# Issuing the attention scores of a head pair as one run of sixteen matmuls instead of two runs of eight

## The chip, the cores and the metric

The kernel runs on one core of a Trainium2 chip. The metric is the time of one execution on the device, in microseconds (us); the median of several executions is quoted, with the lowest and the highest.

## The reference

Two layers in a row. The first is block attention: per head, a sorting matrix `P` (8x8, made by five Sinkhorn steps) mixes the eight blocks of keys and values, then each block attends to itself. The second is a residual MLP whose tokens are mixed too.

```python
# attention: B=4, H=8, S=768, D=64; eight blocks of 96 tokens
k_sorted = np.einsum('bhij,bhjcd->bhicd', P, k_b)
v_sorted = np.einsum('bhij,bhjcd->bhicd', P, v_b)
scores = scale * np.matmul(q_b, k_sb.transpose(0, 1, 2, 4, 3))     # 96x96 per block
attn = softmax(scores); x = np.matmul(attn, v_sb)
# MLP: x is (4, 768, 512)
a1 = alpha1 * x + beta1
tok = np.einsum('ts,bsd->btd', w_tok, a1)                          # token mixing
u = x + lam * tok
ch = np.maximum((alpha2 * u + beta2) @ w_ch1, 0.0) @ w_ch2         # 512 -> 2048 -> 512
out = u + lam * ch
```

## The kernel before

Attention of batch b and the MLP of batch b-1 are emitted one after the other, and a scheduler at build time interleaves them on each engine. TensorE's trace shows the order that was built (batch 1 of before: score runs of 1, 15 and six of 8 in both). The names to know: `sc_ps` are scores, `et` their exps (ScalarE), `x_ps` the value products, `h_ps` the first MLP layer, `ch_ps` its second, `tok_ps` the token mixing. PSUM is split into a pool of two large tiles (`psA`: scores, value products, key and value mixing) and one of four small ones (`psB`: the MLP).

```python
psA = ctx.enter_context(tc.tile_pool(name="psA", bufs=2, space=bass.MemoryType.PSUM))
psB = ctx.enter_context(tc.tile_pool(name="psB", bufs=4, space=bass.MemoryType.PSUM))
# ... cut ...
def emit_scores(b, h4, g, spins=0):                # h4: head pair, g: half of the blocks
    sps = psa([128, 2, 4, 128], FT, "sc_ps")
    # ... cut ...
    for ii, i in enumerate(blocks):                # four blocks
        for h2 in range(2):                        # two heads: rows 0 to 63 and 64 to 127
            rows = slice(h2 * 64, (h2 + 1) * 64)
            pe.matmul(sps[0:BLK, h2, ii, 0:BLK], kT[rows, h4 * NB + i, :],
                      qT[rows, h4, :, i * 16:(i + 1) * 16], start=True, stop=True)
    et = att.tile([BLK, 2, 4, BLK], F16, name="et", tag="et", bufs=4)
    act.activation(et..., sps..., AF.Exp, scale=scale)      # arguments cut
    return et

def emit_attention(b):
    # ... cut ...
    def gather(lo, hi):                            # 96-row blocks into the 128-row layout
        for a in range(3):
            dve.tensor_copy(x128[96:128, a:a + 4:3, lo:hi], xs[32 * a:32 * a + 32, :, lo:hi])

    prev = [emit_scores(b, 0, g) for g in range(2)]
    for h4 in range(1, H4):
        cur = [emit_scores(b, h4, g) for g in range(2)]
        emit_pv(b, h4 - 1, prev, x128, xs)         # value products, then normalised by VectorE
        prev = cur
        if h4 == H4 - 1:
            gather(0, 384)
    emit_pv(b, H4 - 1, prev, x128, xs)
    gather(384, C)

def moe_start(b):                                  # cut to its end
    for kt in range(NT):
        pool.tensor_scalar(u32[kt][:], b1lB[:], rs[:, kt:kt + 1], None, op0=ALU.mult)
        moe_add(b, kt)                             # GpSimd: u = x128 + u

for b in range(1, B):                              # cut to what matters
    emit_attention(b)
    if b == 1:
        moe_ch(0, 0, (2,))
    else:
        moe_h(b - 1, 0)
        moe_ch(b - 1, 0)
    moe_h(b - 1, 1)                                # 64 matmuls
    moe_a(b)                                       # moe_start, token mixing (36 matmuls), transposes
    moe_ch(b - 1, 1)
```

The softmax here doesn't subtract the row's maximum and nothing guards it: scores larger than these inputs give would overflow.

Of the kernel before, what the change touches and what calls it, by code (L numbers as in the profile page):

```python
# [7 lines left out]
FT = mybir.dt.float32  # L8
# [8 lines left out]
def kernel(  # L17
# [23 lines left out]
    NB = sort_net.shape[-1]  # L41
    BLK = S // NB
# [30 lines left out]
    pe = Engine(nc.tensor)  # L73
    dve = Engine(nc.vector)
    act = Engine(nc.scalar)
# [9 lines left out]
    def psa(shape, dtype, name):  # L85
        return psA.tile(shape, dtype, name=name, tag="psA")
# [42 lines left out]
    qT_of = {}  # L129
# [84 lines left out]
    def spin(ps, n):  # L214
        src = ident16[:].unsqueeze(1).to_broadcast([128, 4, 128])
        for _ in range(n):
            pe.matmul(ps, ident16[:], src, start=True, stop=True)
# [104 lines left out]
    kT_of = {}  # L322
# [30 lines left out]
    def mix_k(b, share=(4, 0, 4), gs=range(3)):  # L353
        raw = raw_of[(b, 0)]
        rhs = bigP[b][:].rearrange("p g i -> p (g i)")
        if b not in kT_of:
            kT_of[b] = att.tile([128, H4 * NB, BLK], F16, name="kT", tag="kT", bufs=2)
        kv_ = kT_of[b][:].rearrange("p c (par th tp) -> p th c par tp", th=2, par=2)
        for g in gs:
            kps = psa([128, 8, 128], FT, "k_ps")  # L360
            for tp in range(8):
                t0 = (8 * g + tp) * 128
                pe.matmul(kps[:, tp, :], raw[:, t0:t0 + 128], rhs, start=True, stop=True)
            for par in range(2):
                for h2 in range(2):
                    src = kps[par * 64:(par + 1) * 64, :, h2 * 64:(h2 + 1) * 64].rearrange(
                        "p n (th c) -> p th c n", th=2
                    )
                    dst = kv_[h2 * 64:(h2 + 1) * 64, :, :, par, 8 * g:8 * g + 8]
                    if 2 * par + h2 < share[g]:  # L370
                        dve.tensor_copy(dst, src)
                    else:
                        act.copy(dst, src)

    def mix_heads(kv, h4, out, copies):

# [32 lines left out]

    x_of = {}  # L410

    def emit_scores(b, h4, g, spins=0):
        kT = kT_of[b]
        qT = qT_of[b]
        blocks = ((0, 1, 2, 6), (3, 4, 5, 7))[g] if b == 0 else range(4 * g, 4 * g + 4)
        sps = psa([128, 2, 4, 128], FT, "sc_ps")
        spin(sps[:, 0, :, :].rearrange("p i x -> p (i x)"), spins)
        for ii, i in enumerate(blocks):
            for h2 in range(2):
                rows = slice(h2 * 64, (h2 + 1) * 64)  # L420
                pe.matmul(
                    sps[0:BLK, h2, ii, 0:BLK], kT[rows, h4 * NB + i, :], qT[rows, h4, :, i * 16:(i + 1) * 16],
                    start=True, stop=True,
                )
        et = att.tile([BLK, 2, 4, BLK], F16, name="et", tag="et", bufs=4)
        act.activation(
            et[:].rearrange("p a i (r kt) -> p (a i) r kt", kt=NT),
            sps[0:BLK].rearrange("p a i x -> p (a i) x")[:, :, 0:BLK].rearrange("p n (kt r) -> p n r kt", kt=NT),
            AF.Exp, scale=scale,
        )  # L430
        return et

    def emit_pv(b, h4, ets, x128, xs):
        for g in range(2):
            xall = psa([128, 4, 256], FT, "x_ps")
            xps = xall[0:BLK]
            flat = ets[g][:].rearrange("p a i x -> p (a i x)")
            for ii in range(4):
                i = 4 * g + ii
                for h2 in range(2):  # L440
                    at = (h2 * 4 + ii) * BLK
                    rows = min(128, 8 * BLK - at)
                    pe.matmul(
                        xall[0:rows, ii, h2 * GRP:h2 * GRP + D + 1], flat[:, at:at + rows],
                        Vs[b % NV][:, (2 * h4 + h2) * NB + i, 0:D + 1],
                        start=True, stop=True,
                    )
            recip = att.tile([BLK, 4, 2], FT, name="recip", tag="recip", bufs=3)
            sums = xps[:, :, D:D + GRP + 1:GRP]
            vals = xps[:, :, 0:2 * GRP].rearrange("p i (a g) -> p i a g", a=2)[:, :, :, 0:D]  # L450
            dve.reciprocal(recip[:], sums)
            for lo, hi in ((0, 4),) if g == 0 else ((0, 2), (2, 4)):
                i = 4 * g + lo
                cols = slice(h4 * 128, (h4 + 1) * 128)
                dst = x128[0:BLK, i:i + hi - lo, cols] if i < 6 else xs[:, :, cols]
                dve.tensor_tensor(
                    dst.rearrange("p i (a d) -> p i a d", d=D), vals[:, lo:hi],
                    recip[:, lo:hi].unsqueeze(3).to_broadcast([BLK, hi - lo, 2, D]), ALU.mult,
                )

    def pv_tiles(h4, g, et, spins=0):

# [21 lines left out]
    def emit_attention(b):  # L484
        x128 = moep.tile([128, NT, C], F16, name="x128", tag="x128", bufs=2)
        xs = moep.tile([BLK, 2, C], F16, name="xs", tag="xs", bufs=1)
        x_of[b] = x128

        def gather(lo, hi):
            for a in range(3):  # L490
                dve.tensor_copy(x128[96:128, a:a + 4:3, lo:hi], xs[32 * a:32 * a + 32, :, lo:hi])

        prev = [emit_scores(b, 0, g) for g in range(2)]
        for h4 in range(1, H4):
            cur = [emit_scores(b, h4, g) for g in range(2)]
            emit_pv(b, h4 - 1, prev, x128, xs)
            prev = cur
            if h4 == H4 - 1:
# [3 lines that stand above are left out]
# [171 lines left out]
    def sc0(h4, g, spins=0):  # L673
        ets[(h4, g)] = emit_scores(0, h4, g, spins)
# [83 lines left out]
    for kk in range(2):  # L758
        moe_ch(0, 0, (kk,))
        mix_k(1, gs=((0, 1), (2,))[kk])  # L760
        for h4 in range(2 * kk, 2 * kk + 2):
            turn_q(1, h4, dve.tensor_copy)
    pe.fixed = False
    for b in range(1, B):
        if b > 1:
            if b > 2:
                cross_q(b)
            mixing_matrices(b)
            mix_v(b)
            if b == 2:  # L770
                opened = pool.tensor_copy(gate[:], Vs[0][0:1, 0, 0:2])
                with tc.issue_after(opened.ins):
                    load_q(3)
                    load_raw(3, 1)
                    load_raw(3, 0)
            mix_k(b)
# [6 lines that stand above are left out]
        moe_h(b - 1, 1)  # L783
        moe_a(b)
        moe_ch(b - 1, 1)
        if b == 1:
            load_q(2)
            cross_q(2)
# [33 lines left out]
```

## Time and profile before

| | before |
|---|---|
| time, 3 runs | 269.02 us (268.73 to 269.4) |
| profiled execution | 268.56 us, granted clock 1.00 |
| span in the trace | 266.8 us |
| TensorE busy | 257.3 us (96%) |
| stretch from the first MLP matmul | 219.80 us |

The page of the profile of before, cut to four lines: the span, the busy times (PE is TensorE, PEld its weight loads, DVE VectorE, ACT ScalarE, POOL GpSimd), the chain that ended last by engine, and one group of instructions (count, busy us and mean ns, then idle time before them).

```profile
span 266.8 us, 5147 instructions
...
PE 257.3 (96%) x2049; PEld 141.6 (53%) x2059; DVE 154.8 (58%) x333; ACT 125.8 (47%) x232; POOL 92.6 (35%) x100
...
PE 89%; ACT 4%; DVE 4%; issue 1%; DMA 1%; DVEq 0%; ACTq 0%
...
L65 PE MATMUL h_ps<-a2T,W1p 128*128 128x384 bf16 x512 | 93.4, 326 | 0.2
```

TensorE is the limit nearly everywhere (96% busy, 89% of the chain). The mean of 326 ns is the length of one matmul's record. What a matmul costs the stream is the distance to the next start, 162 ns for an h matmul, so everything below is read start to start.

The timeline of TensorE before, in the middle of batch 3's attention (start, length, engine, operation, output and inputs, count):

```profile
188.76 1.47 PE L65 MATMUL h_ps<-a2T,W1p 128*128 128x384 bf16 x8
190.16 0.38 PE L65 MATMUL sc_ps<-qT,kT 64*96 64x96 f16 x8
190.47 0.50 PE L65 MATMUL h_ps<-a2T,W1p 128*128 128x384 bf16 x2
190.90 0.38 PE L65 MATMUL sc_ps<-qT,kT 64*96 64x96 f16 x8
191.21 0.34 PE L65 MATMUL h_ps<-a2T,W1p 128*128 128x384 bf16 x1
191.50 0.41 PE L65 MATMUL x_ps<-Vs,et 96*128 96x65 f16 x8
```

Scores come in runs of eight and use 64 rows of the array (`64*96`); all their neighbours use 96 or 128. From an h matmul to the first score takes 256 ns instead of 162. From the last score to the next h matmul takes 138.

### The profile page before, as it was taken

What the parts mean: (1) busy time and instruction counts of PE and PEld (TensorE: products, weight loads), DVE (VectorE), ACT (ScalarE), POOL (GpSimd) and SP (SyncE); (2) the same over time, 40 slices, a digit from 0 to 9 for tenths busy, and PEclk for the clock granted to TensorE, in tenths of its full rate; (3) what the DMA queues carried; (4) which work ended last, traced back from release to release, by engine and by line L of the source; (5) the groups of instructions that cost most, each with busy time, mean ns of one, the idle gap of its engine ahead of it and who ended that gap; (6) DMA issues with size and microseconds to landing.
All of it is one profiled execution on the core that took longest, in us unless ns stands there. A gap on an engine that the chain in (4) does not pass through costs nothing.

```text
span 266.8 us, 5147 instructions
## 1 busy us (share of the span) xinstructions
PE 257.3 (96%) x2049; PEld 141.6 (53%) x2059; DVE 154.8 (58%) x333; ACT 125.8 (47%) x232; POOL 92.6 (35%) x100
## 2 busy tenths in 40 slices
PE   7799999999999999999999999999999999999993
PEld 3467745565565444554565444554565445545542
DVE  6878687639567966722585867704675962042033
ACT  3376767642585312980375404970474305505600
POOL 8524789103585615008918125002409000000000
PEclk9999999999999999999999999999999999999999
DMA  6999999989999544499996342492200422012012
GB/s 80 183 208 252 206 211 207 209 209 118 206 165 146 115 83 120 115 83 95 207 196 135 61 100 80 118 109 51 81 1 2 86 71 79 2 39 79 2 39 79
DMA packets 62423, 30.88 MB, mean 116 GB/s; under 512 B 48888, under 2 KB 58112, under 8 KB 62400
## 3 DMA queue, kind: packets, MB, share of 16 engines
q0 software_dynamic: 23024, 15.60, 39.1%
q1 hardware_dynamic: 39376, 14.96, 32.7%
q8 instruction: 16, 0.26, 0.4%
q14 instruction: 7, 0.06, 0.1%
HBM read 32.78 MB, written 8.65 MB: 155 GB/s over the span
## 4 chain that ended last, share of the span: by engine, by line
PE 89%; ACT 4%; DVE 4%; issue 1%; DMA 1%; DVEq 0%; ACTq 0%
PE ch_ps L65 31%; PE h_ps L65 30%; PE tok_ps L65 12%; PE x_ps L65 5%; PE sc_ps L65 4%; ACT kT L65 2%; PE v_ps L65 2%; PE k_ps L65 1%; PE q_ps L65 1%; ACT et L65 1%; DVE csum L65 1%; DVE P L65 1%; PE m_ps L65 1%; DVE rsum L65 1%; PE wtok_ps L65 1%
## 5 line engine op out<-in xcount | busy, mean ns | idle before, releaser
L65 PE MATMUL h_ps<-a2T,W1p 128*128 128x384 bf16 x512 | 93.4, 326 | 0.2
L65 ACT ACTIVATE hTa<-h_ps 128x384 bf16<-128x384 f32 x96 | 45.9, 492 | 67.7 <-PE h_ps L65 66.6
L65 PE MATMUL ch_ps<-W2p,hTa 128*128 128x512 bf16 (+2 forms) x290 | 65.9, 370 | 0.5
L65 PEld LDWEIGHTS <-W1p 128*128 128x128 bf16 x512 | 47.5, 98 | 30.3 <-issue 0.9
L65 DVE TENSOR_TENSOR ch_ps<-ch_ps,lamB 128x512 f32<-128x512 f32 (+2 forms) x25 | 16.9, 676 | 62.8 <-PE ch_ps L65 60.1
L65 POOL TENSOR_SCALAR u<-b1lB,rs 128x512 f32<-128x512 f32 x18 | 28.9, 1612 | 64.7 <-DVE ost L65 60.1
L65 PEld LDWEIGHTS <-hTa 128*128 128x128 bf16 x300 | 28.7, 98 | 32.4
L65 PE MATMUL tok_ps<-x,w_tokT 128*128 128x512 f16 x144 | 32.1, 379 | 0.0
L65 POOL TENSOR_TENSOR u<-x,u 128x512 f32<-128x512 f16 x22 | 25.4, 1190 | 18.2 <-DVE x L65 17.3
L65 ACT ACTIVATE et<-sc_ps 96x768 f16<-96x768 f32 x32 | 24.9, 807 | 11.7 <-PE sc_ps L65 11.7
L65 ACT CAST u<-u 128x512 f16<-128x512 f32 x24 | 14.8, 618 | 25.7 <-DVE u L65 25.7
L65 PE MATMUL ch_ps<-W2p,hTb 128*128 128x512 bf16 (+2 forms) x100 | 25.0, 371 | 0.0
L65 PEld LDWEIGHTS <-w_tokT 128*128 128x128 f16 x180 | 14.8, 97 | 16.1
L65 DVE TENSOR_TENSOR tok_ps<-tok_ps,a1lB 128x512 f32<-128x512 f32 x24 | 16.6, 693 | 7.7 <-PE tok_ps L65 7.6
L65 DVE CAST kT<-k_ps 64x512 f16<-64x512 f32 x24 | 16.5, 688 | 3.4 <-PE k_ps L65 3.0
L65 DVE TENSOR_TENSOR x<-x_ps,recip 96x512 f16<-96x512 f32 (+2 forms) x32 | 17.6, 554 | 0.9
L65 DVE TENSOR_TENSOR u<-tok_ps,u 128x512 f32<-128x512 f32 x24 | 16.4, 689 | 1.7
L65 ACT ACTIVATE hTb<-h_ps 128x384 bf16<-128x384 f32 x32 | 15.3, 497 | 3.8 <-PE h_ps L65 3.4
L65 DVE TENSOR_TENSOR ost<-ch_ps,u 128x512 f32<-128x512 f32 (+2 forms) x25 | 16.6, 665 | 0.6
L65 POOL DMA_DIRECT2D qn<-in_q_dram x18 | 15.4, 872 | 4.2 <-PE q_ps L65 3.4
L65 PEld LDWEIGHTS <-hTb 128*128 128x128 bf16 x100 | 9.6, 98 | 10.9
L65 PEld LDWEIGHTS <-et 96*128 96x128 f16 (+2 forms) x288 | 12.4, 99 | 4.6 <-issue 1.2
(95 smaller groups left out, 214.0 us busy)
## 6 DMA issues: line engine op xcount, KB each, us to landing
out_dram<-ost SPq DMA_DIRECT2D x23, 192.0 KB, 2.2
raw<-in_v_dram POOLq DMA_DIRECT2D x8, 384.0 KB, 8.2
raw<-in_k_dram POOLq DMA_DIRECT2D x8, 384.0 KB, 10.7
vscr<-vA SPq DMA_DIRECT2D x6, 384.0 KB, 4.4
Vs<-vscr SPq DMA_DIRECT2D x6, 384.0 KB, 7.5
W1p<-in_moe_w_ch_dram POOLq DMA_DIRECT2D x4, 512.0 KB, 10.5
W2p<-in_moe_w_ch_dram POOLq DMA_DIRECT2D x4, 512.0 KB, 18.6
qn<-in_q_dram POOLq DMA_DIRECT2D x12, 128.0 KB, 5.8
```

The costliest lines, as they stand in the source:

```text
L65: ins = getattr(self.eng, name)(*args, **kwargs)
```

## The change

The intent is to enter and leave runs of 64-row matmuls half as often. Both PSUM tiles of a head pair are taken first, sixteen score matmuls are issued over them, and then the two exps. The first score waits until both tiles are free (`freed`), and the others are chained to it. Batch 0 keeps its order.

```diff
+    def emit_pair(b, h4):
+
+        pair = [psa([128, 2, 4, 128], FT, "sc_ps") for _ in range(2)]
+        last = None
+        for g in range(2):
+            for ins in score(b, h4, range(4 * g, 4 * g + 4), pair[g]):
+                if last is None:
+                    behind(ins, freed[b], mybir.DependencyClass.Sync)
+                else:
+                    behind(ins, (last,), mybir.DependencyClass.NoSync)
+                last = ins
+        return [emit_exp(ps, b) for ps in pair]
 ... cut: freed[b] is set by the key copies, by each exp and by each normalisation;
 ... cut: emit_scores becomes score (the matmuls) and emit_exp (the exp) ...
-        prev = [emit_scores(b, 0, g) for g in range(2)]
+        prev = emit_pair(b, 0)
         for h4 in range(1, H4):
-            cur = [emit_scores(b, h4, g) for g in range(2)]
+            cur = emit_pair(b, h4)
```

More of the change, by code (lines that the diff above doesn't have):

```diff
@@ L360, in mix_k @@
             kps = psa([128, 8, 128], FT, "k_ps")
+            copies = []
             for tp in range(8):
@@ L370, in mix_k @@
                     if 2 * par + h2 < share[g]:
-                        dve.tensor_copy(dst, src)
+                        ins = dve.tensor_copy(dst, src)
                     else:
-                        act.copy(dst, src)
+                        ins = act.copy(dst, src)
+                    copies.append(ins)
+            freed[b] = copies
     def mix_heads(kv, h4, out, copies):
@@ L410, with score @@
     x_of = {}
-    def emit_scores(b, h4, g, spins=0):
-        kT = kT_of[b]
-        qT = qT_of[b]
-        blocks = ((0, 1, 2, 6), (3, 4, 5, 7))[g] if b == 0 else range(4 * g, 4 * g + 4)
-        sps = psa([128, 2, 4, 128], FT, "sc_ps")
-        spin(sps[:, 0, :, :].rearrange("p i x -> p (i x)"), spins)
+    def score(b, h4, blocks, sps):
         for ii, i in enumerate(blocks):
@@ L420, in emit_scores, with behind, emit_exp @@
                 rows = slice(h2 * 64, (h2 + 1) * 64)
-                pe.matmul(
-                    sps[0:BLK, h2, ii, 0:BLK], kT[rows, h4 * NB + i, :], qT[rows, h4, :, i * 16:(i + 1) * 16],
-                    start=True, stop=True,
-                )
+                yield pe.matmul(
+                    sps[0:BLK, h2, ii, 0:BLK], kT_of[b][rows, h4 * NB + i, :],
+                    qT_of[b][rows, h4, :, i * 16:(i + 1) * 16], start=True, stop=True,
+                )
+    freed = {}
+    def behind(ins, others, kind):
+        for other in others:
+            tc.add_manual_dep(
+                ins.ins, other.ins.name, mybir.DependencyInfo(kind, mybir.DependencyReason.DATA), reason="scores"
+            )
+    def emit_pair(b, h4):
[9 more added lines that the diff above has]
+        return [emit_exp(ps, b) for ps in pair]
+    def emit_scores(b, h4, g, spins=0):
+        sps = psa([128, 2, 4, 128], FT, "sc_ps")
+        spin(sps[:, 0, :, :].rearrange("p i x -> p (i x)"), spins)
+        for _ in score(b, h4, ((0, 1, 2, 6), (3, 4, 5, 7))[g], sps):
+            pass
+        return emit_exp(sps)
+    def emit_exp(sps, b=0):
         et = att.tile([BLK, 2, 4, BLK], F16, name="et", tag="et", bufs=4)
-        act.activation(
+        freed[b] = [act.activation(
             et[:].rearrange("p a i (r kt) -> p (a i) r kt", kt=NT),
@@ L429, in emit_scores @@
             AF.Exp, scale=scale,
-        )
+        )]
         return et
@@ L455, in emit_pv @@
                 dst = x128[0:BLK, i:i + hi - lo, cols] if i < 6 else xs[:, :, cols]
-                dve.tensor_tensor(
+                freed[b] = [dve.tensor_tensor(
                     dst.rearrange("p i (a d) -> p i a d", d=D), vals[:, lo:hi],
                     recip[:, lo:hi].unsqueeze(3).to_broadcast([BLK, hi - lo, 2, D]), ALU.mult,
-                )
+                )]
     def pv_tiles(h4, g, et, spins=0):
```

## The prediction

> **What bounds the kernel.** The matmul stream: the busy table gives TensorE 257.3 of 266.8 us (96%), the chain of waits 89% TensorE, the clock row full speed throughout. So only TensorE's slots, switches and waits count. In the attention of batches 1 to 3 (66 to 82, 114 to 139, 173 to 198 us in the timeline) score and value matmuls are slipped in between the MLP's.
>
> **What a visit to the scores costs (trace, start to start).** h matmuls follow each other at 162 ns; h to first score takes 256, which is 94 more. Last score to h takes 138, though inside a run score pairs take 3 and 42 ns: about 96 more. Scores use 64 rows, the others 128. [...] The second pair of a run also starts 35 ns late. So an unhindered run of 8 costs 405 ns, of 15 581, of one 266 (read), of 16 about 585 (estimate).
>
> **What the change does.** No matmul, exp or copy is added or removed. The built order shows eight score runs per batch before (1, 15, six of 8), four of 16 after. Unhindered: 266 + 581 + 6x405 = 3277 ns becomes 4x585 = 2340 per batch; 2.8 us less in three batches, all on the critical path.
>
> **What it gives back.** Both PSUM tiles of the pool of two are filled at once and handed to ScalarE together. An exp takes 807 ns, two back to back start some 700 apart, so the second ends about 1.5 us after the pair. Between a later pair and the value group that needs the first tile back stand only 3 h matmuls (0.49 us), and 2 before the next group. Before, the exps were staggered, and such waits were 0.12 to 0.19 us, about twice per batch. I stepped both orders through with durations, slots and hand-over delays (37 ns TensorE to ScalarE, 50 back) read from the trace: waits of about 0.3 + 0.14 us after each of the two mid-attention pairs of a batch, 0.25 at the second pair's start; 1.9 us more waiting in all, mostly value group after h. Net estimate: batch 1 about even (+0.1), batches 2 and 3 together -0.85; total -0.75 us. Other moves (batch 2's mixing matrices earlier, its key mixing in one run of 16) hardly change TensorE's sum.
>
> **Predicted time: 268.3 us, range 267.3 to 269.2.** Faster by over 2%: 0.01; within 2%: 0.98; slower by over 2%: 0.01.
>
> **What the profile would show.** Right: 12 score runs of 16, each with one 94 ns entry and one 138 ns exit; a pair's exps adjacent on ScalarE, 0.7 us apart; value groups starting 50 ns after an exp's end, with 0.1 to 0.4 us lost after h matmuls; batch 1's attention as long as before, the other two 0.4 us shorter each; the MLP-only tail unchanged. Wrong: no new gaps before value groups (the gain nears 2.5 us), or gaps at score entries beyond 0.3 us.
>
> **What would make it wrong.** If the pair's exps queue behind more Relu evictions (491 ns each) than I count, waits grow and the change is even or slower, up to +0.5 us. If the second tile of a run starts late, the gain shrinks. If waits are hidden better, 266.5 us. The gain is near the spread of the runs of before (268.73 to 269.4).

The sum: +0.1 us for batch 1 and -0.85 for batches 2 and 3, -0.75 in all.

## More of the kernel before

Because the effect is a few tenths of a percent, I also use a length read from each trace: the **stretch**, from the start of the first MLP matmul (at about 43 us) to the start of the last matmul. Ahead of it lie DMA loads and the unchanged batch 0.

The end of batch 1's attention before, on TensorE, VectorE and GpSimd:

```profile
80.76 0.43 PE L65 MATMUL x_ps<-Vs,et 96*128 96x65 f16 x8
...
81.02 4.23 PE L65 MATMUL h_ps<-a2T,W1p 128*128 128x384 bf16 x25
...
83.58 1.61 DVE L65 COPY x<-xs 32x256 f16<-32x256 f16 x3
83.95 4.53 POOL L65 TENSOR_TENSOR u<-x,u 128x512 f32<-128x512 f16 x4 [3.27 <-DVE x L65]
...
85.09 2.75 PE L65 MATMUL tok_ps<-x,w_tokT 128*128 128x512 f16 x12
```

After the last value group at 80.76, VectorE normalises and gathers until 85.19, and token mixing needs the result. TensorE has 25 h matmuls to do meanwhile and starts token mixing at 85.09 without a gap.

## The result, and the profile after

| | before | after |
|---|---|---|
| time, 6 runs each | 269.15 us (268.73 to 269.4) | 269.53 us (269.15 to 275.12) |
| ratio, 95% interval | | 1.0012 (0.9998 to 1.0027) |
| span in the trace | 266.8 us | 268.1 us |
| TensorE busy | 257.3 us | 255.3 us |
| stretch from the first MLP matmul | 219.80 us | 220.42 us |

A ratio is the mean time of one kernel's runs over that of the other's of the same rounds, so it is not quite the ratio of the medians. Executions over 1.5% slower than the fastest of the same kernel are left out of the means. The time is outside the predicted range (267.3 to 269.2), and the stretch became longer by 0.62 us where a gain was forecast. Of the 1.3 us between the two spans, 0.69 lies ahead of the stretch, where both programs are the same.

The page of the profile after, cut to the same lines but for the group of instructions:

```profile
span 268.1 us, 5145 instructions
...
PE 255.3 (95%) x2048; PEld 141.1 (53%) x2059; DVE 155.4 (58%) x333; ACT 126.3 (47%) x232; POOL 92.3 (34%) x100
...
PE 71%; DMA 12%; ACT 6%; POOL 5%; DVE 4%; issue 2%; POOLq 0%; ACTq 0%; DVEq 0%
```

TensorE is busy for 2 us less. The chain's larger share of DMA must not be read as the change's doing: 24.2 us of it (9% of the span) are two weight loads between 7.5 and 32 us, ahead of the stretch, where both programs are the same. What differs inside the stretch is in the view of waits for TensorE after (what waited, for what: total us, times, longest):

```profile
PE tok_ps L65 <- DVE x L65: 1.0, 2, 0.8
PE x_ps L65 <- ACT et L65: 0.8, 4, 0.2
...
PE sc_ps L65 <- ACT et L65: 0.3, 2, 0.2
PE k_ps L65 <- ACT kT L65: 0.3, 1, 0.3
```

Before has none of these four. This view counts a wait only from where the modelled end of the last matmul lies, so each is smaller than the loss start to start. The timeline after, in the middle of batch 3's attention (the bracket is the idle time and what ended it):

```profile
191.92 0.56 PE L65 MATMUL sc_ps<-qT,kT 64*96 64x96 f16 x16
192.41 0.66 PE L65 MATMUL h_ps<-a2T,W1p 128*128 128x384 bf16 x3
193.26 0.41 PE L65 MATMUL x_ps<-Vs,et 96*128 96x65 f16 x8 [0.19 <-ACT et L65]
193.51 0.49 PE L65 MATMUL h_ps<-a2T,W1p 128*128 128x384 bf16 x2
193.97 0.41 PE L65 MATMUL x_ps<-Vs,et 96*128 96x65 f16 x8
```

ScalarE in the same place:

```profile
192.03 0.49 ACT L65 ACTIVATE hTa<-h_ps 128x384 bf16<-128x384 f32 x1 [0.16 <-PE h_ps L65]
192.42 1.50 ACT L65 ACTIVATE et<-sc_ps 96x768 f16<-96x768 f32 x2
```

Both exps end 1.5 us after the first begins. Only three h matmuls and then two fill the time, and the value groups lose 0.35 and 0.12 us start to start. Now the end of batch 1's attention after:

```profile
83.26 0.42 PE L65 MATMUL x_ps<-Vs,et 96*128 96x65 f16 x8
83.52 2.28 PE L65 MATMUL h_ps<-a2T,W1p 128*128 128x384 bf16 x13
...
85.91 1.61 DVE L65 COPY x<-xs 32x256 f16<-32x256 f16 x3
86.19 0.62 PE L65 MATMUL tok_ps<-x,w_tokT 128*128 128x512 f16 x2 [0.26 <-DVE x L65]
86.28 3.45 POOL L65 TENSOR_TENSOR u<-x,u 128x512 f32<-128x512 f16 x3 [5.28 <-DVE x L65]
...
87.57 1.67 PE L65 MATMUL tok_ps<-x,w_tokT 128*128 128x512 f16 x7 [0.76 <-DVE x L65]
```

Here are 13 h matmuls, not 25. Token mixing starts while the gather is unfinished, and its third matmul comes 1138 ns after its second instead of 216. In all, 1.28 us are lost ahead of and inside it: 0.33, 0.03 and 0.92.

Single records show where the gather's time goes. The first two copies take 0.22 us each. The third takes 1.11 us, from 86.41 to 87.52, and GpSimd's first add runs from 86.28 to 87.44. The copy ends 0.08 us after the add, here as in before (85.19 and 85.11). That the add holds it up was inferred from this; pair_adds_wait, below, tests it. The traces of both kernels have such a third copy (1.10 to 1.11 us) in each of batches 1 to 3. Only where it is uncovered does it cost anything: in batch 1, 0.92 us in this trace and nothing in that of before.

The balance of the 0.62 us, from start-to-start distances in both traces:

| | before | after | difference |
|---|---|---|---|
| score runs of batches 1 to 3, entry and exit and waits included | 10.40 us | 7.99 us | -2.40 |
| waits ahead of and in value groups | 0.79 us | 2.78 us | +1.99 |
| waits ahead of and in batch 1's token mixing | 0 | 1.28 us | +1.28 |
| all the rest (key mixing, MLP slots) | | | -0.25 |

The last row is the remainder and was not followed. (The traces of before and after lack 10 and 11 of 2059 matmul records; the distances, summed, do not depend on them.)

### The profile page after: what moved, and what is told of

Same layout as the page of the kernel before. It is cut to its first block, busy times and chain, and to the rows that moved or that the text cites. A ratio compares the mean times of both kernels' runs of the same rounds, so it can differ in the third digit from the quotient of the medians.

```text
span 268.1 us, 5145 instructions
## 1 busy us (share of the span) xinstructions
PE 255.3 (95%) x2048; PEld 141.1 (53%) x2059; DVE 155.4 (58%) x333; ACT 126.3 (47%) x232; POOL 92.3 (34%) x100
## 4 chain that ended last, share of the span: by engine, by line
PE 71%; DMA 12%; ACT 6%; POOL 5%; DVE 4%; issue 2%; POOLq 0%; ACTq 0%; DVEq 0%
PE ch_ps L65 30%; PE h_ps L65 24%; PE tok_ps L65 9%; DMA wt<-in_moe_w_tok_dram 6%; DMA W1p<-in_moe_w_ch_dram 3%; ACT et L65 3%; DMA qn<-in_q_dram 3%; PE x_ps L65 2%; POOL qn L65 2%; ACT kT L65 2%; PE v_ps L65 2%; PE k_ps L65 1%; PE sc_ps L65 1%; POOL raw L65 1%; DVE kT L65 1%
## 5 line engine op out<-in xcount | busy, mean ns | idle before, releaser
L65 PE MATMUL h_ps<-a2T,W1p 128*128 128x384 bf16 x512 | 91.9, 326 | 0.1
L65 PEld LDWEIGHTS <-et 96*128 96x128 f16 (+2 forms) x288 | 13.0, 99 | 7.1 <-issue 3.5
L65 PE MATMUL x_ps<-Vs,et 96*128 96x65 f16 (+2 forms) x288 | 14.7, 194 | 1.0 <-ACT et L65 0.8
```

Of the source, the lines that this page charges most:

```text
L65: ins = getattr(self.eng, name)(*args, **kwargs)
```

## The experiments

Theory A: the pairing saves and gives back as forecast, but its longer waits made the scheduler spend h matmuls earlier, so too few were left to cover the end of batch 1's attention. Theory B: the loss is in the exps and the PSUM tiles handed over together, wherever pairs stand. Theory C: chance of one execution.

| run | time, us | ratio to before (95%) | stretch, us |
|---|---|---|---|
| before | 268.96 and 268.79 (11 runs in each group) | | 219.80 |
| after_again | 270.04 | 1.0019 (0.9988 to 1.005) | 220.43 |
| pair_adds_wait | 269.34 | 1.0008 (0.9963 to 1.0053) | 219.54 |
| pair_ch_first | 269.53 | 1.001 (0.9981 to 1.0039) | 220.32 |
| before_short_tail | 269.6 | 1.0018 (0.9994 to 1.0042) | 220.65 |
| pair_batches_23 | 268.29 | 0.9975 (0.9954 to 0.9996) | 219.29 |
| pair_batch_1 | 270.44 | 1.0068 (1.0022 to 1.0114) | 221.65 |
| pair_ch_mix | 270.14 | 1.0042 (1.0019 to 1.0065) | 221.34 |
| pair_long_tail | 272.73, one run | | 222.44 |
| before_adds_wait | 269.21, one run | | 219.80 |

The first four runs after `before` form one group on one chip, the next three and `pair_long_tail` a second; `before_adds_wait` ran alone on a third, beside one run of before of 270.69 us. Every result was correct. Most ratios settle nothing by themselves, and the verdicts rest on the stretches, each from one profiled fast execution (for the two single runs the state is unknown). In `pair_batch_1`, `pair_ch_mix` and `pair_ch_first` the fastest execution's span was 1.2, 0.5 and 1.7 us shorter than the traced one's. A start as early as 42.44 us, the earliest in the traces, would explain 0.6, 0.1 and 1.4 us of that, so their stretches hold at least some 0.6, 0.4 and 0.3 us that not every execution had.

### after_again: the changed kernel once more

No edit.

> The changed kernel once more, as the control of this group. Both theories: 0.0 to +0.5 us against before. The wait of TensorE ahead of and inside the first token-mixing group of batch 1 (1.28 us in the first profile of it) returns at the same size if it is the order's doing (theory A); it is gone or much different if it was chance of one execution (theory C). Theory C also says that the 0.7 us by which its first profile was late before 43 us, where the two programs are the same, comes from chance and moves from run to run.

The stretch came out at 220.43 us against 220.42, and the waits at token mixing were the same to 10 ns. The stretch began at 43.42 us instead of 43.16. (In this trace the granted clock also stood at half from 14.35 to 17.76 us, ahead of the stretch; TensorE had been busy for 2.15 of the 3.42 us before that.) Theory C is out for the loss inside the stretch; for the lateness ahead of it, it fits.

### pair_adds_wait: GpSimd's adds held back in batch 1

```diff
-                moe_add(b, kt)
+                add = moe_add(b, kt)
+                if b == 1:
+                    behind(add, (gathered[b],), mybir.DependencyClass.Sync)   # the last gather copy
```

> Changed kernel, but GpSimd's six adds onto batch 1's attention output wait for the last of VectorE's three gather copies. TensorE's order is unchanged. Theory A (the pairing used up the MLP matmuls that hid the end of batch 1's attention; its last link is a gather copy of 1.1 us that stands still behind GpSimd's add): that copy falls to about 0.22 us, the third token-mixing gap from 1138 to about 250 ns, the kernel is 0.8 to 0.9 us faster than the changed kernel, about 0.5 below before. Theory B (the loss is the exps' and the two PSUM tiles' hand-over, the tail is hidden): within 0.2 us of the changed kernel.

The third copy took 0.22 us, the third token-mixing gap fell from 1138 to 250 ns, and the stretch was 0.88 us shorter than the changed kernel's. That is 0.26 us below before, where about 0.5 was forecast. The timeline of VectorE, GpSimd and TensorE in this run:

```profile
85.19 0.72 DVE L65 COPY x<-xs 32x256 f16<-32x256 f16 x3
...
86.06 3.49 POOL L65 TENSOR_TENSOR u<-x,u 128x512 f32<-128x512 f16 x3 [5.78 <-DVE x L65]
...
85.46 1.74 PE L65 MATMUL tok_ps<-x,w_tokT 128*128 128x512 f16 x7 [0.26 <-DVE x L65]
```

The three copies take 0.72 us instead of 1.61, and the second idle bracket of TensorE is gone. Theory A holds. The copy's delay beside the add is 0.88 us of the wait, and about 0.4 us remain because 13 matmuls don't cover the rest of VectorE's chain.

### before_adds_wait: the same edit on the kernel before

> The kernel before, with batch 1's six GpSimd adds made to wait for the last gather copy, as in the run on the changed kernel that gained 0.88 us. Theory A: that copy falls from 1.1 to about 0.22 us here too, but 25 MLP matmuls already hide it, so the stretch from the first MLP matmul to the last matmul stays at 219.80 us within 0.1. If the copy cost time wherever it stood long, it would be some 0.9 us shorter.

The third copy fell to 0.22 us and the stretch stayed at 219.80 us. The long copy costs nothing while 25 matmuls cover it.

### before_short_tail: the uncovered end without any pairing

```diff
+            moe_h(0, 1, range(13))
+            finish()                       # the last value group of batch 1 and its gather
...
-        moe_h(b - 1, 1)
+        moe_h(b - 1, 1, range(13, HT) if b == 1 else range(HT))
```

> The kernel before, its score runs untouched (8 per batch, none paired), but 13 of the 25 MLP matmuls that follow batch 1's last value group are issued ahead of that group, so that 12 follow. No matmul added. Theory A: a wait of 1.1 to 1.4 us before and in batch 1's token mixing, and 0.8 to 1.3 us slower than before, without any pairing. Theory B: within 0.3 us of before.

The stretch grew by 0.85 us, to 220.65, with the score runs of before. The timeline of TensorE:

```profile
83.65 2.12 PE L65 MATMUL h_ps<-a2T,W1p 128*128 128x384 bf16 x12
85.69 0.20 PE L65 MATMUL rep_ps<-P,ebh 32*128 32x64 f16 x1
85.83 0.61 PE L65 MATMUL tok_ps<-x,w_tokT 128*128 128x512 f16 x2
87.11 1.24 PE L65 MATMUL tok_ps<-x,w_tokT 128*128 128x512 f16 x5 [0.68 <-DVE x L65]
```

The wait for the third copy stands at the same place. The lost cover alone brings it about. It is 0.85 us and not the 1.1 to 1.4 that were forecast: the loss of 0.33 us ahead of token mixing did not appear, so no run shows that part without pairing.

### pair_batches_23 and pair_batch_1: the change by parts

```diff
+        if not (b > 1):          # pair_batches_23; in pair_batch_1: not (b == 1)
+            ... two runs of eight, each with its exp, as before
```

> The change in batches 2 and 3 alone; batch 1 keeps the order of before (built order: identical up to batch 2's scores, 25 MLP matmuls in batch 1's tail). Read in the stretch from the first MLP matmul to the last matmul of the trace (before 219.80 us, changed 220.42 and 220.43), since executions differ by up to 1.4 us ahead of it. Theory A (pairing is worth about 0.3 to 0.45 us a batch; batch 1 alone loses, by its uncovered tail): 218.9 to 219.2, that is 0.6 to 0.9 us below before and 1.2 to 1.5 below the changed kernel, no wait above 0.3 us before token mixing. Theory B (pairing loses wherever it stands, by the exps): 220.0 or more.

> The change in batch 1 alone. Same stretch. Theory A: 221.0 to 221.3, that is 1.2 to 1.5 us above before, with the 1.28 us of waits before and in batch 1's token mixing as in the changed kernel, and dearer than the change in all three batches. Theory B: between before and the changed kernel, 219.9 to 220.2.

In batches 2 and 3 alone, the change shortened the stretch by 0.51 us, to 219.29, somewhat less than forecast (218.9 to 219.2). The median was 268.29 us against 268.79, with a ratio whose interval lies below 1. This version is ahead of before in time by 0.25%, and its stretch is shorter than those of both kernels; it was not run beside the changed kernel. Its token mixing of batch 1 starts without a wait:

```profile
81.82 3.74 PE L65 MATMUL h_ps<-a2T,W1p 128*128 128x384 bf16 x22
85.39 1.46 PE L65 MATMUL tok_ps<-x,w_tokT 128*128 128x512 f16 x6
```

(The other three of its 25 h matmuls stand merged with earlier ones.) In batch 1 alone, the change lengthened the stretch by 1.85 us, more than forecast. The waits at token mixing were as expected. A wait of 0.71 us ahead of a value group of batch 2 appeared as well, in this run only. It accounts for the difference between the parts' sum (1.85 - 0.51 = 1.34) and the whole (0.62). Two lines of the timeline show what ended it:

```profile
134.96 0.69 DVE L65 TENSOR_TENSOR ost<-ch_ps,u 128x512 f32<-128x512 f32 x1 [0.93 <-DMA out_dram<-ost]
...
136.36 0.42 PE L65 MATMUL x_ps<-Vs,et 96*128 96x65 f16 x8 [0.54 <-DVE xs L65]
```

VectorE stood still for 0.93 us until an output transfer had left the buffer of `ost`, and the normalisation (`xs`) that the value group waits for came after that. In before_short_tail VectorE works in the same order there and does not wait. With the shorter spans of other executions, this looks like a late transfer of this one execution and not like a cost of pairing; no second trace shows it. Without it, batch 1 alone would stand at +1.14 us, close to the forecast of 1.2 to 1.5. Theory B is out as an account of the loss: pairing gains in two batches and loses in one.

### pair_ch_first and pair_ch_mix: covering the end with output matmuls

```diff
         moe_h(b - 1, 1)
+        if b == 1:
+            mixing_matrices(2)             # only in pair_ch_mix
+            moe_ch(b - 1, 1, (0,))
         moe_a(b)
-        moe_ch(b - 1, 1)
+        moe_ch(b - 1, 1, (1, 2) if b == 1 else range(3))
```

> Changed kernel, with one of the three output-matmul groups of batch 0 (16 ch matmuls, 3.45 us) emitted ahead of batch 1's token mixing, to cover the tail with work. The built order shows it there, and batch 2's start as in before. Theory A: no gap before the token mixing of batch 1; 1.1 to 1.4 us faster than the changed kernel, 0.7 to 1.0 us below before. Theory B: within 0.3 us of the changed kernel.

> The run with output matmuls ahead of batch 1's token mixing lost its gain in a wait of 1.17 us of the value mixing of batch 2 on VectorE's late mixing matrices. Here those matrices are emitted earlier, ahead of the moved output matmuls, where VectorE is free. If that wait was the whole of what went missing: no gap over 0.4 us before token mixing, no wait over 0.2 us before the value mixing, stretch 219.1 to 219.5 us, 0.9 to 1.3 below the changed kernel and 0.3 to 0.7 below before. If the moved matmuls cost something else, 219.9 or more.

Both forecasts of a gain were wrong. In the first, the gap ahead of token mixing was gone, but the stretch was only 0.10 us shorter than the changed kernel's, since a new wait stood in front of batch 2's value mixing:

```profile
104.69 2.45 PE L65 MATMUL h_ps<-a2T,W1p 128*128 128x384 bf16 x14
...
108.14 1.04 PE L65 MATMUL v_ps<-raw,bigV 128*128 128x512 f16 x4 [1.01 <-DVE bigV L65]
```

With the mixing matrices made earlier, the wait turned up one step later, at the key mixing (1.88 us start to start), and the stretch grew to 221.34 us:

```profile
104.39 1.25 DVE L65 TENSOR_SCALAR a2T<-a2T,ab2col 128x384 bf16<-128x384 f16 x4 [2.88 <-DMA a2T<-u]
105.55 0.69 DVE L65 TENSOR_TENSOR ch_ps<-ch_ps,lamB 128x512 f32<-128x512 f32 x1
...
106.28 0.69 DVE L65 TENSOR_TENSOR ost<-ch_ps,u 128x512 f32<-128x512 f32 x1
...
106.88 1.21 DVE L65 CAST vA<-v_ps 128x1024 f16<-128x1024 f32 x1
...
108.15 1.05 PE L65 MATMUL k_ps<-bigP,raw 128*128 128x128 f16 x16 [1.72 <-DVE vA L65]
```

VectorE first stands still for 2.88 us until a transposing transfer (`a2T<-u`) has landed, then empties the output matmuls' tile, and only then the value mixing's own, which key mixing waits for. The same wait on the transfer is 1.87 us in the changed kernel and 2.22 us in pair_ch_first. So in both runs the wait moved along VectorE's work and was not removed. How much of it is the order's doing and how much a late transfer of the one execution is not shown; the ratio of pair_ch_mix, above 1 with its whole interval, says that the order is at any rate no gain.

### pair_long_tail: more matmuls kept for the end

```diff
+                if (b, hf) == (0, 1) and m >= HT - 6 and ci == 0:
+                    behind(ins, (tail[1],), mybir.DependencyClass.NoSync)   # last value matmul of batch 1
```

> Changed kernel with 24 MLP matmuls (instead of 13) held behind batch 1's last value group. In the built order they are taken from between the value groups. Theory A adds that the MLP matmuls are one fixed supply: the token mixing's wait vanishes (under 0.3 us), but waits of 0.4 to 0.6 us appear at each of the last four value groups; the stretch is 0.2 to 1.2 us longer than the changed kernel's (estimate by stepping the order through: +1.1), not shorter. A rival by which the tail alone is at fault: 1.0 us or more shorter.

Token mixing no longer waited, and the last four value groups lost 0.51, 0.45, 0.49 and 0.63 us. The supply is fixed, as theory A adds. The stretch was 2.02 us longer than the changed kernel's, more than forecast, and the rest has another cause. TensorE by stretches of 3.4 us in this run (busy us and count, granted clock, DMA share, GB/s):

```profile
77.60:81.00 3.40, 3.28 (x45) 1.00 1.06 166
81.00:84.40 3.40, 1.98 (x35) 0.98 2.18 189
84.40:87.80 3.40, 3.40 (x12) 0.52 1.99 109
87.80:91.20 3.40, 3.40 (x21) 1.00 0.69 139
```

After a stretch in which TensorE was busy for 1.98 of 3.40 us, the clock fell to half for 3.41 us. Ten h matmuls took 158 ns longer each and one 73: 1.65 us. Some 0.4 us is left for the waits themselves, inside the forecast of 0.2 to 1.2. What brought the half clock on is not shown: in after_again the clock stood at half after TensorE was busy for 2.15 of 3.42 us, but in pair_ch_mix it stayed full after 2.10 of 3.41 us (106.84 to 110.25).

## Why the prediction was wrong

- **What bounds the kernel: right.** The balance above is TensorE's slots, switches and waits, and it accounts for the 0.62 us but for 0.25.
- **The saving: right.** The changed kernel has twelve runs of 16. Seven of them cost 584 or 585 ns, as estimated, and the other five carry waits of 0.10 to 0.24 us at their entry. Less those waits, the saving is 3 x (3277 - 4 x 585) ns, 2.8 us. A merge of two runs of eight saves 2 x 405 - 585 = 225 ns: the 94 ns of an entry, the 96 of an exit and the 35 of a late second pair, as read in the trace of before.
- **What it gives back: right in place, the sum somewhat too small.** Forecast were 0.3 + 0.14 us at the value groups after each mid-attention pair; the trace has 0.29 to 0.35 and 0.12. In all, 1.9 us more waiting was forecast. The value groups alone wait 1.99 us more, and the score entries add 0.4 (2.8 us saved unhindered against 2.40 in the balance), so some 0.5 us of the error stands here. This is read from the trace. No run took the exps' load away.
- **Batches 2 and 3: right in sign, too large.** Forecast was -0.85 us; pairing there alone gave -0.51.
- **The step that failed is "batch 1 about even (+0.1)", together with "Other moves [...] hardly change TensorE's sum".** I weighed the moves of MLP matmuls by their own slots, which don't change. I did not ask what they had been hiding. The 12 that went forward had covered the last 2 us of a VectorE chain of some 4 us, which the token mixing needs. Without them, 1.28 us came to light; before_short_tail brings 0.85 of it about without pairing, and pair_batches_23 avoids it. Batch 1 alone cost 1.85 us instead of 0.1, of which 0.71 stood in batch 2 behind a late transfer.
- **The size inside that step.** In stepping through I took the copies of the last gather at their median, 0.22 us (the prediction does not say so). The trace of before had one of 1.11 us in each of batches 1 to 3, beside GpSimd's first add. pair_adds_wait puts this at 0.88 us; before_adds_wait shows why it was worth nothing before.
- **What stays open.** Some executions of the changed kernel took over 274 us, 3 of 12. Before had none so slow in its 6, 11 and 11. No trace of one was kept.

## What to carry to other kernels

Merging small switches on a saturated engine saved here what was forecast of it, but it also changed when the filler work was used, and filler is a fixed supply. Before moving matmuls, find each long chain on other engines that they cover, measure it at its slowest instruction rather than at the median, and count how many will be left over it. Apply such a change per stage: here the version that pairs only in batches 2 and 3 came out 0.25% ahead of before, with the shortest stretch of all runs.
